# Attention, expert layer and MLP on one core: the conversion of doubles moved between engines, the first expert started in blocks of 128 tokens

## The chip, the cores and the metric

One core of a Trainium2 chip runs the whole program. The engines are TensorE (PE in the profile; PEld is its weight load), VectorE (DVE), ScalarE (ACT), GpSimd (POOL) and SyncE (SP), which issues most DMAs. Each runs its own instructions in order. The metric is the device time of one execution in microseconds (us); lower is better.

## The reference, cut to what matters

```python
def reference(**kwargs):
...
    attn_out = _attn_ref(**attn_kwargs)
    B, H, S, D = attn_out.shape
    x = np.ascontiguousarray(attn_out.transpose(0, 2, 1, 3)).reshape(B * S, H * D)
    x = _moe_ref(x=x, **moe_kwargs)
    return _moe2_ref(x=x, **moe2_kwargs)
```

Attention has batch 4, 8 heads, 768 positions of 64 features; a query sees 96 local and 8 global keys, with a linear bias. Its rows (3072 tokens of 512 features) are dealt to 8 experts of 384 tokens each by a greedy rule over the gate's logits; an expert is `relu(x @ w1) @ w2` with 1024 hidden features. A last MLP (`w_in`, a leaky relu with its own slope per feature, `w_out`, 2048 hidden features) runs over all tokens. The results of the random generators times constants are doubles for `w_in` and `w_out`, so these two arrive in 64 bits and the kernel makes float32 of them.

## The kernel before, in words

**Attention and conversion.** `attention` goes through 24 tiles of 128 queries, each in two steps of four heads (u = 0 and 1), so through 48 steps, and a step's parts are written in an order by hand. In step n: DMA issues for later tiles on SP; `place_globals` copies the global keys into the key columns of step n + 2 (POOL, L190); `place_values` copies the global values into rows of the value tile before (POOL, L196); then scores of step n + 1 (PE L212, DVE L218, ACT L221), the transposes of the probabilities (PE L232, copies on DVE L236 and ACT L234), the divisor (POOL L259), the combination of step n - 2 (PE L277, DVE), transposes of keys or queries for a later tile (PE L169, ACT L174 or L178), and last the product with the values of step n - 1 (PE L248).

Beside it runs `Doubles`, a generator of 32 jobs that turns 128x512 doubles into floats. `turn(n)` gives it four steps of five, two calls of `next(side)` in such a step. At the first call `begin` puts the shifted and limited high word into `t` (ACT L73, POOL L74) and the scaled low word into `r` (POOL L75), and `finish` splits the job before into a high and a low part if it belongs to `w_in`, every second job (POOL L87, L88). At the second call, the step's end, `join` packs the bits (DVE L79, L80) and adds the low word (POOL L82). `t` and `r` have two buffers, the raw tile three; the load of a raw tile is issued in `begin`'s call, two jobs ahead.

**Router and experts.** After attention the `Router` searches for the expert and its 384 tokens by counting above thresholds (DVE, with small matmuls). It is a generator too, and `filler` (L404) is a row of bf16 matmuls whose result nobody reads, put on PE between. `Experts.run` gathers the first expert's rows in three indirect DMAs of 128 tokens (POOL), transposes them (PE L857), splits them into a high and a low part (ACT L872, DVE L873), and runs the products in three passes (high by high, high by low, low by high). The first layer is `up1` (L923), with its relu on ACT and DVE (L926, L927), then `down1` (L950). Weights are split by `split` (ACT L890, POOL L891). Only the first expert's start is changed; later experts are transposed inside the previous expert's second layer (`up2` L963, `down2` L988).

The loop that sets the step's order:

```python
            if n + 2 < N:
                place_globals(*steps[n + 2])
            place_values(g, u)
            if turn(n):
                next(side)
            if nx:
                scores(*nx)
...
        if turn(n):
            next(side)
        else:
            next(setup, None)
```

Of the kernel before, what the change touches and what calls it, by code (L numbers as in the profile page):

```python
# [9 lines left out]
FT = mybir.dt.float32  # L10
FR = mybir.dt.float32r
BF = mybir.dt.bfloat16
I32 = mybir.dt.int32
U32 = mybir.dt.uint32
U16 = mybir.dt.uint16
AF = mybir.ActivationFunctionType
OP = mybir.AluOpType
# [13 lines left out]
class Doubles:  # L31
# [37 lines left out]
    def begin(self, job):  # L69
        nc, raw = self.nc, job["raw"]  # L70
        t = job["t"] = self.pool.tile([128, self.WIDTH], I32, name="f64_t")
        r = job["r"] = self.pool.tile([128, self.WIDTH], I32, name="f64_r")
        nc.scalar.activation(t.bitcast(FT), raw[:, :, 1].bitcast(FT), AF.Abs, scale=LIFT)  # L73
        nc.gpsimd.tensor_scalar(t.bitcast(FT), t.bitcast(FT), BIG, FLOOR, op0=OP.min, op1=OP.max)  # L74
        nc.gpsimd.tensor_scalar(r, raw[:, :, 0].bitcast(U32), 2.0 ** -29, 1.0, op0=OP.mult, op1=OP.mult)  # L75

    def join(self, job):
        nc, t = self.nc, job["t"]
        nc.vector.tensor_scalar(t, t, 3, 0x7FFFFFF8, op0=OP.logical_shift_left, op1=OP.bitwise_and)  # L79
        nc.vector.scalar_tensor_tensor(t, job["raw"][:, :, 1], -0x80000000, t, op0=OP.bitwise_and, op1=OP.bitwise_or)  # L80
        dst = t if job["dst"] is None else job["dst"].bitcast(I32)
        nc.gpsimd.tensor_tensor(dst, t, job["r"], op=OP.add)  # L82

# [7 lines left out]
def attention(ctx, tc, q, k, v, w_gate, n_global, n_local, ident, x_dram, logits, side, router):  # L91
# [212 lines left out]
    def turn(n):  # L304
        return 2 <= n < N - 3 and n % PACE[1] < PACE[0]
# [14 lines left out]
    for n in range(N + 2):  # L320
        if n < N:
# [8 lines left out]
            if n + 2 < N:  # L330
                place_globals(*steps[n + 2])
            place_values(g, u)
            if turn(n):
# [20 lines left out]
        if n >= N:  # L354
            combine(*steps[n - 2])
        if turn(n):
            next(side)
        else:
            next(setup, None)


class Router:
# [236 lines left out]
    def phase(self, k, result):  # L599
# [116 lines left out]
        if wide:  # L716
            self.filler(5120)
        yield
# [80 lines left out]
class Experts:  # L799
# [86 lines left out]

    def split(self, name, e, f, shape):
        r = self.st.pop(("r" + name, e, f))
        s = self.pair("m_s" + name, shape, 2)
        self.nc.scalar.activation(s[:, 0], r, AF.Copy)  # L890
        self.nc.gpsimd.tensor_tensor(s[:, 1], r, s[:, 0], op=OP.subtract)  # L891
        self.st["s" + name, e, f] = s
# [22 lines left out]
    def up1(self, e, f):  # L915
        nc = self.nc
        s1 = self.st.pop(("s1", e, f))
        x = self.ex[e]["x"]
        n = self.NT * 128
        ps = self.hidden.tile([128, 512], FT, name="m_h", bufs=3)  # L920
        for d in range(self.ND):
            for i, (a, b) in enumerate(self.PASSES):
                nc.tensor.matmul(ps[:, :n], s1[:, a, d], x[:, b, d], start=(d == 0 and i == 0),  # L923
                                 stop=(d == self.ND - 1 and i == 2))
        h = self.pair("m_hh", [n], 2)
        nc.scalar.activation(h[:, 0], ps[:, :n], AF.Relu)  # L926
        nc.vector.scalar_tensor_tensor(h[:, 1], ps[:, :n], 0.0, h[:, 0], op0=OP.max, op1=OP.subtract)  # L927
        self.st["h", e, f] = h

    @staticmethod  # L930
# [75 lines left out]
    def run(self, router, n_experts):  # L1006
# [15 lines left out]
        self.load_rest(0)  # L1022
        self.split_w1(0, 0)
        next(gen)
        ps = [self.acc.tile([128, 512], FT, name="m_acc", bufs=4) for _ in range(self.ND)]
        for a in range(self.NT):
            for d in range(self.ND):
                self.transpose(ps[d], 0, a, d)
        for d in range(self.ND):
            self.x_split(ps[d], 0, d)  # L1030
        self.split_w1(0, 1)
# [13 lines left out]

        self.up1(0, 0)
        next(gen)
# [133 lines left out]
```

## Time and profile before

| what | value |
|---|---|
| runs of the kernel before | 1121.75 us median of 3 (1120.18 to 1121.84) |
| the profiled execution | 1119.95 us, its span 1118.2 us |
| busy share of the span | PE 95%, PEld 84%, DVE 68%, POOL 48%, ACT 34% |
| mean granted TensorE clock | 0.976 of full speed |

The span runs from the first to the last instruction; the profiled execution's time holds 1.75 us more that lies around it. PE is busy nearly everywhere, but the matmuls' ends are modelled, and PE can be slow while busy: PEclk tells the clock that it was granted. The share of an engine over the whole span mixes attention, where DVE, POOL and ACT are well filled, with the expert part, where PE is.

### The profile page before, as it was taken

What the parts mean: (1) busy time and instruction counts of PE and PEld (TensorE: products, weight loads), DVE (VectorE), ACT (ScalarE), POOL (GpSimd) and SP (SyncE); (2) the same over time, 40 slices, a digit from 0 to 9 for tenths busy, and PEclk for the clock granted to TensorE, in tenths of its full rate; (3) what the DMA queues carried; (4) which work ended last, traced back from release to release, by engine and by line L of the source; (5) the groups of instructions that cost most, each with busy time, mean ns of one, the idle gap of its engine ahead of it and who ended that gap; (6) DMA issues with size and microseconds to landing.
All of it is one profiled execution on the core that took longest, in us unless ns stands there. A gap on an engine that the chain in (4) does not pass through costs nothing.

```text
span 1118.2 us, 19406 instructions
## 1 busy us (share of the span) xinstructions
PE 1065.7 (95%) x6659; PEld 944.2 (84%) x6659; DVE 762.9 (68%) x2228; ACT 385.6 (34%) x969; POOL 540.5 (48%) x652
## 2 busy tenths in 40 slices
PE   8989898869999999999999999999999999999997
PEld 6777677648888998899889988898899999999995
DVE  7989888778897878897789698778753323231321
ACT  7777777503322320232133113211331233123211
POOL 4888878315455823462346325432543354236222
PEclk9999999968999999999999999999999999999999
DMA  9788877114135525441534533533353435434131
GB/s 219 212 218 223 209 202 187 49 46 134 57 132 179 173 83 181 130 160 58 198 96 149 163 123 109 157 135 129 95 180 123 133 108 185 131 116 167 57 131 67
DMA packets 151219, 156.55 MB, mean 140 GB/s; under 512 B 83536, under 2 KB 116304, under 8 KB 151120
## 3 DMA queue, kind: packets, MB, share of 16 engines
q1 hardware_dynamic: 147280, 142.72, 42.3%
q0 software_dynamic: 3840, 12.59, 3.4%
q8 instruction: 53, 0.87, 0.3%
q14 instruction: 46, 0.38, 0.1%
HBM read 134.31 MB, written 20.97 MB: 139 GB/s over the span
## 4 chain that ended last, share of the span: by engine, by line
PE 75%; DVE 12%; POOL 6%; issue 3%; ACT 2%; DMA 2%; SPq 0%; DVEq 0%; POOLq 0%; ACTq 0%
PE m_h L963 23%; PE m_acc L988 23%; PE m_h L923 9%; PE m_acc L950 9%; PE a_s L212 2%; PE a_pt L232 2%; PE a_xp L248 2%; DVE r_thr L564 2%; DVE r_red L778 1%; DVE r_cmp L770 1%; PE r_ps L704 1%; POOL wo L82 1%; ACT a_p L221 1%; PE a_cb L277 1%; PE a_tp L169 1%
## 5 line engine op out<-in xcount | busy, mean ns | idle before, releaser
L973 POOL TENSOR_TENSOR m_g<-m_t,m_g 128x384 fp32r<-128x384 f32 (+1 forms) x144 | 140.2, 973 | 372.1 <-ACT m_g L972 369.1
L988 PE MATMUL m_acc<-m_so,m_g 128*128 128x512 f32 x1152 | 298.7, 399 | 0.4 <-POOL m_spacer L996 0.3
L963 PE MATMUL m_h<-m_y,wi 128*128 128x384 f32 x1536 | 294.4, 341 | 0.0
L963 PEld LDWEIGHTS m_h<-m_y,wi 128*128 128x128 f32 x1536 | 273.3, 189 | 7.5
L988 PEld LDWEIGHTS m_acc<-m_so,m_g 128*128 128x128 f32 x1152 | 209.6, 189 | 35.3 <-POOL m_g L973 0.9
L972 ACT ACTIVATE m_g<-m_t 128x384 fp32r<-128x384 f32 (+1 forms) x144 | 70.5, 490 | 435.6 <-DVE m_t L971 255.1
L891 POOL TENSOR_TENSOR m_s<-m_r,m_s 128x512 fp32r<-128x512 f32 x128 | 166.9, 1308 | 103.5 <-ACT m_s L890 103.2
L970 DVE TENSOR_SCALAR m_t<-m_h,m_al 128x384 f32<-128x384 f32 (+1 forms) x144 | 82.2, 571 | 149.2 <-PE m_h L963 136.1
L950 PE MATMUL m_acc<-m_hh,m_s 128*128 128x384 f32 x768 | 150.3, 340 | 1.3 <-DVE m_hh L927 1.3
L923 PE MATMUL m_h<-m_xt,m_s 128*128 128x384 f32 x768 | 146.1, 338 | 0.0
L923 PEld LDWEIGHTS m_h<-m_xt,m_s 128*128 128x128 f32 x768 | 136.4, 190 | 1.9 <-ACT m_xt L872 0.3
L950 PEld LDWEIGHTS m_acc<-m_hh,m_s 128*128 128x128 f32 x768 | 132.4, 188 | 2.9 <-DVE m_hh L927 1.6
L890 ACT ACTIVATE m_s<-m_r 128x512 fp32r<-128x512 f32 x128 | 79.7, 626 | 98.8 <-PE m_acc L950 34.1
L221 ACT ACTIVATE a_p<-a_sx,a_mn 128x232 f32<-128x232 f32 (+1 forms) x192 | 88.5, 462 | 25.8 <-DVE a_mn L218 25.4
L927 DVE SCALAR_TENSOR_TENSOR m_hh<-m_h,m_hh 128x384 fp32r<-128x384 f32 x64 | 35.4, 552 | 76.8 <-ACT m_hh L926 76.2
L971 DVE SCALAR_TENSOR_TENSOR m_t<-m_h,m_t 128x384 f32<-128x384 f32 (+1 forms) x144 | 73.9, 513 | 4.9
L778 DVE TENSOR_REDUCE r_red<-r_cmp 128x24 bf16<-128x576 bf16 (+1 forms) x97 | 73.9, 761 | 3.4
L218 DVE CUSTOM_DVE_ANT_0 a_sx<-a_s,a_bias 128x232 f32<-128x232 f32 (+1 forms) x192 | 61.4, 374 | 11.6 <-PE a_s L212 9.4
L212 PE MATMUL a_s<-a_kz,a_qz 64*128 64x232 f32 (+1 forms) x384 | 50.2, 381 | 18.7 <-POOL a_kz L190 16.2
L926 ACT ACTIVATE m_hh<-m_h 128x384 fp32r<-128x384 f32 x64 | 31.5, 492 | 95.6 <-PE m_h L923 82.3
L770 DVE TENSOR_TENSOR r_cmp<-r_mk,r_thr 128x576 bf16<-128x576 uint16 x78 | 61.4, 787 | 0.0
L212 PEld LDWEIGHTS a_s<-a_kz,a_qz 64*128 64x128 f32 x384 | 33.2, 193 | 28.6 <-POOL a_kz L190 22.6
(183 smaller groups left out, 1283.3 us busy)
## 6 DMA issues: line engine op xcount, KB each, us to landing
m_so<-wo_pairs SPq DMA_DIRECT2D x112, 512.0 KB, 3.3
m_r<-in_moe_w_dram SPq DMA_DIRECT2D x128, 256.0 KB, 3.0
f_raw<-in_moe_w_in_dram SPq DMA_DIRECT2D x16, 512.0 KB, 4.6
f_raw<-in_moe_w_out_dram SPq DMA_DIRECT2D x16, 512.0 KB, 3.7
wo_pairs<-m_so SPq DMA_DIRECT2D x16, 512.0 KB, 2.6
a_k<-in_k_dram SPq DMA_DIRECT2D x24, 256.0 KB, 4.8
a_q<-in_q_dram SPq DMA_DIRECT2D x24, 256.0 KB, 5.2
a_v<-in_v_dram SPq DMA_DIRECT2D x24, 256.0 KB, 4.8
```

The source lines that it names most:

```text
L212: nc.tensor.matmul(ps[s][:, a, :n], T["Q", g][r, p], kz[r, p, c0:c0 + n], start=True, stop=True)
L221: nc.scalar.activation(pr[:, s, 2 * C - n:], sx[:, s, :n], AF.Exp, bias=T["mn", g][:, h:h + 1], scale=-1.0, accum_out=T["sum", g][:, h:h + 1])
L778: nc.vector.tensor_reduce(red, cmp, axis=AX.X, op=OP.add)
L890: self.nc.scalar.activation(s[:, 0], r, AF.Copy)
L891: self.nc.gpsimd.tensor_tensor(s[:, 1], r, s[:, 0], op=OP.subtract)
L923: nc.tensor.matmul(ps[:, :n], s1[:, a, d], x[:, b, d], start=(d == 0 and i == 0), stop=(d == self.ND - 1 and i == 2))
L950: nc.tensor.matmul(ps[:, :n], s2[:, b, d * 128:(d + 1) * 128], h[:, a], start=(f == 0 and a + b == 0), stop=(last and a == 1))
L963: nc.tensor.matmul(ps[:, :n], self.wi[:, a, d, f * 128:(f + 1) * 128], y[:, b, d], start=(d == 0 and i == 0), stop=(d == self.ND - 1 and i ...
L970: nc.vector.tensor_scalar(t[:, cs], ps[:, cs], 0.0, self.al[:, f:f + 1], op0=OP.min, op1=OP.mult)
L971: nc.vector.scalar_tensor_tensor(t[:, cs], ps[:, cs], 0.0, t[:, cs], op0=OP.max, op1=OP.add)
L973: nc.gpsimd.tensor_tensor(g[:, 1, cs], t[:, cs], g[:, 0, cs], op=OP.subtract)
L988: nc.tensor.matmul(ps, g[:, a, t * 128:(t + 1) * 128], s[:, b], start=(f == 0 and a + b == 0), stop=(last and a == 1))
```

## The change

Four things change. In `Doubles`, the scaling of the low word is an ACT pass that writes back into the raw tile, `r` is gone, the add reads the raw tile, and `t` has three buffers. In `attention`, `place_values` is called at the step's end, ahead of the second call of the side work. In the router one row of filler is 6144 columns long instead of 5120. And the first expert's start is a function of its own, `first_up`: each block of 128 tokens is transposed into one bank, split in one pass, and multiplied by itself in 12 matmuls of 128 columns; two fillers of 512 columns stand between; the first split of `w1` has its subtraction on DVE, and the router's next step and the other splits come after.

```diff
--- before.py
+++ after.py
@@ -68,18 +68,17 @@
 
     def begin(self, job):
         nc, raw = self.nc, job["raw"]
-        t = job["t"] = self.pool.tile([128, self.WIDTH], I32, name="f64_t")
-        r = job["r"] = self.pool.tile([128, self.WIDTH], I32, name="f64_r")
+        t = job["t"] = self.pool.tile([128, self.WIDTH], I32, name="f64_t", bufs=3)
         nc.scalar.activation(t.bitcast(FT), raw[:, :, 1].bitcast(FT), AF.Abs, scale=LIFT)
         nc.gpsimd.tensor_scalar(t.bitcast(FT), t.bitcast(FT), BIG, FLOOR, op0=OP.min, op1=OP.max)
-        nc.gpsimd.tensor_scalar(r, raw[:, :, 0].bitcast(U32), 2.0 ** -29, 1.0, op0=OP.mult, op1=OP.mult)
+        nc.scalar.activation(raw[:, :, 0], raw[:, :, 0].bitcast(U32), AF.Copy, scale=2.0 ** -29)
 
     def join(self, job):
         nc, t = self.nc, job["t"]
         nc.vector.tensor_scalar(t, t, 3, 0x7FFFFFF8, op0=OP.logical_shift_left, op1=OP.bitwise_and)
         nc.vector.scalar_tensor_tensor(t, job["raw"][:, :, 1], -0x80000000, t, op0=OP.bitwise_and, op1=OP.bitwise_or)
         dst = t if job["dst"] is None else job["dst"].bitcast(I32)
-        nc.gpsimd.tensor_tensor(dst, t, job["r"], op=OP.add)
+        nc.gpsimd.tensor_tensor(dst, t, job["raw"][:, :, 0], op=OP.add)
 
     def finish(self, job):
         if job["hi"] is not None:
@@ -329,7 +328,6 @@
             nx = steps[n + 1] if n + 1 < N else None
             if n + 2 < N:
                 place_globals(*steps[n + 2])
-            place_values(g, u)
             if turn(n):
                 next(side)
             if nx:
@@ -353,6 +351,8 @@
             router.start()
         if n >= N:
             combine(*steps[n - 2])
+        if n < N:
+            place_values(g, u)
         if turn(n):
             next(side)
         else:
@@ -714,7 +714,7 @@
         ps = self.psum.tile([128, 512], FT, name="r_ps")
         nc.tensor.matmul(ps[:, :3], lists.rearrange("p g s -> p (g s)"), self.unit, start=True, stop=True)
         if wide:
-            self.filler(5120)
+            self.filler(6144)
         yield
         idx = w.tile([128, 3], I32, name="r_idx", bufs=8)
         nc.vector.tensor_copy(idx, ps[:, :3])
@@ -884,11 +884,11 @@
         self.nc.sync.dma_start(r, src[:, f, :])
         self.st["r2", e, f] = r
 
-    def split(self, name, e, f, shape):
+    def split(self, name, e, f, shape, engine=None):
         r = self.st.pop(("r" + name, e, f))
         s = self.pair("m_s" + name, shape, 2)
         self.nc.scalar.activation(s[:, 0], r, AF.Copy)
-        self.nc.gpsimd.tensor_tensor(s[:, 1], r, s[:, 0], op=OP.subtract)
+        (engine or self.nc.gpsimd).tensor_tensor(s[:, 1], r, s[:, 0], op=OP.subtract)
         self.st["s" + name, e, f] = s
 
     def split_w1(self, e, f):
@@ -922,10 +922,49 @@
             for i, (a, b) in enumerate(self.PASSES):
                 nc.tensor.matmul(ps[:, :n], s1[:, a, d], x[:, b, d], start=(d == 0 and i == 0),
                                  stop=(d == self.ND - 1 and i == 2))
+        self.relu(ps, e, f)
+
+    def relu(self, ps, e, f):
+        nc, n = self.nc, self.NT * 128
         h = self.pair("m_hh", [n], 2)
         nc.scalar.activation(h[:, 0], ps[:, :n], AF.Relu)
         nc.vector.scalar_tensor_tensor(h[:, 1], ps[:, :n], 0.0, h[:, 0], op0=OP.max, op1=OP.subtract)
         self.st["h", e, f] = h
+
+    def first_up(self, filler):
+        nc = self.nc
+        s1 = self.st.pop(("s1", 0, 0))
+        x = self.ex[0]["x"] = self.pair("m_xt", [self.ND, self.NT * 128], 1)
+        out = self.hidden.tile([128, 512], FT, name="m_h", bufs=3)
+
+        def part(a):
+            return slice(a * 128, (a + 1) * 128)
+
+        def turn(a):
+            ps = self.acc.tile([128, 512], FT, name="m_acc", bufs=4)
+            for d in range(self.ND):
+                nc.tensor.transpose(ps[:, part(d)], self.ex[0]["xr"][a][:, part(d)], self.ident)
+            ps = ps.rearrange("p (d t) -> p d t", t=128)
+            hi, lo = x[:, 0, :, part(a)], x[:, 1, :, part(a)]
+            nc.scalar.activation(hi, ps, AF.Copy)
+            nc.vector.tensor_tensor(lo, ps, hi, op=OP.subtract)
+
+        def multiply(a):
+            todo = [(d, i, j) for i, j in self.PASSES for d in range(self.ND)]
+            todo.sort(key=lambda m: m[2])
+            for n, (d, i, j) in enumerate(todo):
+                nc.tensor.matmul(out[:, part(a)], s1[:, i, d], x[:, j, d, part(a)], start=(n == 0),
+                                 stop=(n == len(todo) - 1))
+
+        turn(0)
+        filler(512)
+        turn(1)
+        multiply(0)
+        turn(2)
+        multiply(1)
+        filler(512)
+        multiply(2)
+        self.relu(out, 0, 0)
 
     @staticmethod
     def order(n, last):
@@ -1020,14 +1059,8 @@
         nc.gpsimd.iota(behind, pattern=[[0, 1]], base=0, channel_multiplier=0)
         nc.sync.value_load(behind[0:1, 0:1], min_val=0, max_val=1)
         self.load_rest(0)
-        self.split_w1(0, 0)
-        next(gen)
-        ps = [self.acc.tile([128, 512], FT, name="m_acc", bufs=4) for _ in range(self.ND)]
-        for a in range(self.NT):
-            for d in range(self.ND):
-                self.transpose(ps[d], 0, a, d)
-        for d in range(self.ND):
-            self.x_split(ps[d], 0, d)
+        self.split("1", 0, 0, [self.ND, 128], nc.vector)
+        self.first_up(router.filler)
         self.split_w1(0, 1)
         self.split_w2(0, 0)
         self.split_w2(0, 1)
@@ -1043,7 +1076,7 @@
             else:
                 self.split_w2(e, 1)
 
-        self.up1(0, 0)
+        next(gen)
         next(gen)
         self.split_w1(0, 2)
         chosen = fetched = 0
```

POOL, in attention, two steps in a row of which the second finishes a `w_in` job (a_kz the keys with the global ones placed, a_v the values, a_se the divisor, f_t and f_r the two words of a job, wi and wo the resident weights). Before:

```order
L259 TENSOR_SCALAR a_se<-a_sum 128x4
L190 COPY a_kz<-a_kg 128x2x8
L196 COPY a_v<-a_vg 32x256
L74 TENSOR_SCALAR f_t<-f_t 128x512
L75 TENSOR_SCALAR f_r<-f_raw 128x512
L87 TENSOR_SCALAR wi<-f_t 128x512
L88 TENSOR_TENSOR wi<-f_t,wi 128x512
L259 TENSOR_SCALAR a_se<-a_sum 128x4
L82 TENSOR_TENSOR wo<-f_t,f_r 128x512
```

With the change (line numbers are one less):

```order
L258 TENSOR_SCALAR a_se<-a_sum 128x4
L195 COPY a_v<-a_vg 32x256
L189 COPY a_kz<-a_kg 128x2x8
L73 TENSOR_SCALAR f_t<-f_t 128x512
L86 TENSOR_SCALAR wi<-f_t 128x512
L87 TENSOR_TENSOR wi<-f_t,wi 128x512
L258 TENSOR_SCALAR a_se<-a_sum 128x4
L195 COPY a_v<-a_vg 32x256
L81 TENSOR_TENSOR wo<-f_t,f_raw 128x512
```

The copy into a_v has moved behind the divisor, right ahead of the add of the same step, and the instruction that made f_r is gone; the add reads f_raw.

PE, the first expert's start (m_x gathered rows, m_xt their split transposes, m_s a split weight, m_acc and m_h PSUM banks). Before:

```order
L857 MATMUL m_acc<-ident,m_x 128x128 x12
L923 MATMUL m_h<-m_xt,m_s_4034 128x384 x12
L786 LDWEIGHTS r_ones
L786 MATMUL r_ps<-r_red,r_ones 128x24
L923 MATMUL m_h<-m_xt,m_s_4076 128x384 x12
```

With the change:

```order
L946 MATMUL m_acc<-ident,m_x 128x128 x4
L404 LDWEIGHTS r_ones
L404 MATMUL m_h<-r_slots,r_ones 128x512
L946 MATMUL m_acc<-ident,m_x 128x128 x4
L956 MATMUL m_h<-m_xt,m_s_4004 128x128 x12
L946 MATMUL m_acc<-ident,m_x 128x128 x4
L956 MATMUL m_h<-m_xt,m_s_4004 128x128 x12
L404 LDWEIGHTS r_ones
L404 MATMUL m_h<-r_slots,r_ones 128x512
L956 MATMUL m_h<-m_xt,m_s_4004 128x128 x12
```

The twelve transposes and twelve wide matmuls have become three times four transposes and three times twelve narrow ones, the second block's transposes ahead of the first block's matmuls, with a filler (L404) in two places.

ACT at the same place (m_r a loaded weight tile, m_hh the hidden rows). Before:

```order
L890 ACTIVATE m_s_4034<-m_r_3927 128x512
L872 ACTIVATE m_xt<-m_acc 128x384 x4
L890 ACTIVATE m_s_4076<-m_r_3931 128x512
L890 ACTIVATE m_s_4079<-m_r_3929 128x512
L890 ACTIVATE m_s_4082<-m_r_4028 128x512
L926 ACTIVATE m_hh<-m_h 128x384
```

With the change:

```order
L890 ACTIVATE m_s_4004<-m_r_3895 128x512
L949 ACTIVATE m_xt<-m_acc 128x4x128 x3
L930 ACTIVATE m_hh<-m_h 128x384
L890 ACTIVATE m_s_4073<-m_r_3899 128x512
L890 ACTIVATE m_s_4076<-m_r_3897 128x512
L890 ACTIVATE m_s_4079<-m_r_3998 128x512
```

The relu (m_hh) now stands ahead of the three splits of the next weights, which stood ahead of it before.

## Rows read from the trace of the kernel before

**Rows 1.** Windows, five attention steps each: length, busy us per engine, clock, DMA, GB/s.
```profile
114.70:136.63 21.93, 17.84 (x169) 14.22 (x165) 18.86 (x75) 16.65 (x55) 18.66 (x31) 1.00 0.83 218
...
sum 179.83, PE 160.83 PEld 132.49 DVE 154.71 ACT 137.32 POOL 149.96; mean PE 20.10 PEld 16.56 DVE 19.34 ACT 17.17 POOL 18.75
```

**Rows 2.** Timeline, DVE, first score reduction of four steps: start us, us, engine.
```profile
118.15 0.40 DVE L218 CUSTOM_DVE_ANT_0 a_sx<-a_s,a_bias 128x232 f32<-128x232 f32 x1 [1.01 <-PE a_s L212]
...
122.41 0.39 DVE L218 CUSTOM_DVE_ANT_0 a_sx<-a_s,a_bias 128x232 f32<-128x232 f32 x1
...
131.13 0.39 DVE L218 CUSTOM_DVE_ANT_0 a_sx<-a_s,a_bias 128x232 f32<-128x232 f32 x1
...
136.63 0.39 DVE L218 CUSTOM_DVE_ANT_0 a_sx<-a_s,a_bias 128x232 f32<-128x232 f32 x1
```

**Rows 3.** Waits, 40 to 206 us: us in total, times, longest.
```profile
PEld a_s L212 <- POOL a_kz L190: 22.1, 18, 3.0
ACT a_p L221 <- DVE a_mn L218: 20.8, 26, 2.0
ACT f_t L73 <- POOL wi L88: 20.5, 11, 3.1
...
POOL a_v L196 <- PE a_xp L248: 2.7, 4, 0.9
```

**Rows 4.** Readers of the raw doubles, 40 to 206 us: ns minimum/median/maximum.
```profile
L75 POOL TENSOR_SCALAR f_r<-f_raw x29: 659/681/954, 39.4 to 197.4; 128x512 int32<-128x512 uint32 x29
L80 DVE SCALAR_TENSOR_TENSOR f_t<-f_raw,f_t x29: 691/1020/1643, 40.4 to 197.8; 128x512 int32<-128x512 int32 x29
L73 ACT ACTIVATE f_t<-f_raw x28: 654/674/703, 42.6 to 193.7; 128x512 f32<-128x512 f32 x28
```

**Rows 5.** Timeline, PE, one attention step.
```profile
138.36 1.05 PE L212 MATMUL a_s<-a_kz,a_qz 64*128 64x232 f32 x8
...
140.28 0.66 PE L277 MATMUL a_cb<-a_cmb,a_xt 128*128 128x144 f32 x4
140.77 0.60 PE L169 MATMUL a_tp<-ident,a_k 128*128 128x128 f32 x4
...
142.32 1.05 PE L212 MATMUL a_s<-a_kz,a_qz 64*128 64x232 f32 x8
```

**Rows 6.** Timeline, PE, the first expert's start.
```profile
252.52 0.95 PE L857 MATMUL m_acc<-ident,m_x 128*128 128x128 f32 x4 [0.95 <-DMA m_x<-x_rows,r_idx]
254.08 1.11 PE L857 MATMUL m_acc<-ident,m_x 128*128 128x128 f32 x4 [0.61 <-DMA m_x<-x_rows,r_idx]
255.14 4.48 PE L923 MATMUL m_h<-m_xt,m_s 128*128 128x384 f32 x12
...
259.51 2.37 PE L923 MATMUL m_h<-m_xt,m_s 128*128 128x384 f32 x12
261.72 1.72 PE L950 MATMUL m_acc<-m_hh,m_s 128*128 128x384 f32 x9
```

**Rows 7.** Timeline, ACT and POOL, the same stretch.
```profile
256.09 1.69 ACT L890 ACTIVATE m_s<-m_r 128x512 fp32r<-128x512 f32 x3
259.65 0.49 ACT L926 ACTIVATE m_hh<-m_h 128x384 fp32r<-128x384 f32 x1 [1.87 <-PE r_ps L786]
...
256.82 3.77 POOL L891 TENSOR_TENSOR m_s<-m_r,m_s 128x512 fp32r<-128x512 f32 x3 [4.37 <-ACT m_s L890]
```

**Rows 8.** Windows, the first expert's start.
```profile
253.00:256.00 3.00, 2.39 (x9) 1.35 (x8) 1.59 (x4) 1.41 (x4) 0.00 (x0) 0.50 0.85 234
```

**Rows 9.** Timeline, PE, the second layer of a later expert.
```profile
563.58 2.37 PE L963 MATMUL m_h<-m_y,wi 128*128 128x384 f32 x12
565.79 1.55 PE L988 MATMUL m_acc<-m_so,m_g 128*128 128x512 f32 x6
567.18 0.19 PE L786 MATMUL r_ps<-r_red,r_ones 128*128 128x24 bf16 x1
```

**Rows 10.** Windows, from the first expert's second product to the end.
```profile
261.72:1118.20 856.48, 842.48 (x4569) 764.77 (x4568) 550.94 (x1390) 216.63 (x422) 369.01 (x353) 0.99 0.39 130
```

## The prediction

> **What bounds the kernel now.** I read the windows view first. From the first expert's second product on, PE is busy in 842.5 of 856.5 us [rows 10]. The change touches nothing in that last part, and nothing there can move but PE's own work, so I take its 856.5 us as they are. What can move lies before it: attention with the conversion of the doubles, and the first expert's start.
>
> In attention I cut the time into groups of five steps, because a conversion job runs in four steps of five. Eight groups take 179.83 us, 22.48 each [rows 1]. No engine is full: the means are PE 20.1, DVE 19.3, POOL 18.75, ACT 17.2. The steps are unequal: one takes 4.26 us (118.15 to 122.41), another 5.50 (131.13 to 136.63) [rows 2]. The waits tell who makes the long ones: ACT waits 20.5 us in all for POOL's low-part subtraction L88 before it may write the next t (two buffers), and PE's weight loads wait 22.1 us for the key copies L190 that stand behind that work in POOL's queue [rows 3]. A job whose two parts are written out puts L74, L75, L87, L88 and L82 on POOL in one step; POOL falls behind, ACT stands at L73 ahead of the exponentials, and the next step is long.
>
> At the first expert's start PE transposes three blocks of gathered rows as they land, waits for the split of x, and runs its first product, 12 matmuls, from 255.14 to 259.51 [rows 6]. It does so at a granted clock of 0.50, the 1.2 GHz level [rows 8]; the second product takes 2.21 us, half as long, at 259.51 [rows 6].
>
> **Attention, part by part.** (1) The multiplication of the low words leaves POOL, 0.681 us at the median, and comes to ACT as a pass like L73, 0.674 us [rows 4]. The trace has no such ACT pass with integers, so L73, the same shape and the same stride, is its price. Per group of four jobs POOL goes from 18.75 to 16.0 us, ACT from 17.17 to 19.9. (2) DVE's L80 takes 0.691 us at best and 1.020 at the median [rows 4]; part of that is POOL beside it. With less on POOL, DVE's 19.3 falls to between 18.0 (four times 0.33 less) and 19.3. (3) The third t buffer lets L73 write while the job two before is still being split: the 20.5 us wait of ACT goes. What is late next is ACT itself, now the fullest with 19.9. (4) The copy of the values waits at the head of POOL's step for PE's product, 2.7 us in all [rows 3]; at the end of the step that product is past, and the wait is covered. Behind it in the queue now stands only the add L82, which waits for DVE anyway; the values are needed one step later, so I price the move at nothing; if PE's product were late again, it would cost those 2.7 us. (5) On SP the load of a raw tile now waits for POOL's add, not for DVE's L80, about 1.3 us later; it is needed two jobs, some 8 us, on. Nothing, unless it holds k, q and v behind it (a rival below).
>
> What is a group then? PE's dense step is 3.96 us (138.36 to 142.32) [rows 5], five of them 19.8. I take a step with a job at 4.26, the step of [rows 2] in which nobody stood long, and the fifth at PE's 3.96: 4 x 4.26 + 3.96 = 21.0. That leaves ACT 1.1 us of slack in a group, which is tight. The gain is 22.48 - 21.0 = 1.48, times 8 groups **-11.8 us**. Ends: ACT's 19.9 as the whole group gives -20.6; if 32 new passes, 21.6 us, stay on the path and only the wait of 20.5 goes, +1.1. I stay nearer the good end since three of the four steps of [rows 2] already run at 4.26 to 4.36 (122.41 to 131.13 are two).
>
> Here a rule of the Trainium skill speaks about (2). The row shows L80 0.33 us above its best at the median [rows 4]. The page "SBUF — State Buffer", where it reads the diagram of the ports, says that VectorE with two SBUF inputs and GpSimd lock one another out for whole instructions. By it the removed 0.681 could give DVE up to 4 x 0.681 = 2.7 us a group, and the sum would be at the good end, -20.6; the constant 0.33 does not look like it, and no step here shows it alone.
>
> **The first expert's start.** (6) The fillers of 6144 columns are two matmuls more, while PE only waits for rows: nothing. (7) The first product becomes 36 matmuls of 128 columns instead of 12 of 384, block by block. No such narrow product in this number format is in the trace. By columns: 384 take 2.21/12 = 0.184 us and 512 take 1.39/6 = 0.232 [rows 9], so 128 would take 0.088. By the nearest width in plain fp32: two 144-wide products take 0.49 us [rows 5], 0.218 for 128. I take 0.218, since width is what changes here and only that row has it. The second block's rows are transposed by about 253.1. Then 12 x 0.218 gives 255.7, the third block's transposes 256.2, twelve more 258.8, a filler 259.0, twelve more 261.6, against 259.51 before [rows 6]: +2.1 us. This is at the full clock, 2.4 GHz: the fillers and the early blocks leave fewer gaps than the transposes alone did; that the clock stays up no row can tell. (8) The split of w1 for the second product moves behind the relu on ACT. Before, ACT did three splits in 1.69 us at 256.09 and POOL three subtractions in 3.77 at 256.82, all under the slow first product, and the relu came at 259.65 [rows 7]. Now POOL's part is done only about 2.6 us after the first product (relu 0.4, split 0.56, subtraction 1.26, and 0.35 for three hand-overs, estimated from the gaps between those rows), and PE can do two matmuls before: a new stall of 2.2 us. The down product's own split is then ready in time. (9) The first split's subtraction on DVE runs while rows are on their way: nothing. (10) The router's next pass on DVE comes after the relu; PE reaches its total only after the second product, covered. Sum **+4.3 us**. Ends: with 0.088 the first product ends at 257.0, so -2.5 + 2.2 = -0.3; with 0.218 and the half clock up to 259.5 as before, 6.4 us do 3.2 of 8.55 us of work, the end is 264.9, +7.5.
>
> **Sum.** -11.8 + 4.3 = -7.5. The profiled execution took 1119.95 us (span 1118.2), so 1112.45; the median of the runs is 1.80 above it: **1114.2 us**.
>
> **Rivals.**
> - The narrow products go by columns (0.088). For it: 384 and 512 lie on one line [rows 9]. Then -11.8 - 0.3 = -12.1, 1109.7 us. The Trainium skill, "TensorE: Matmul & The Clock Gate", section on the back-to-back issue gap, gives 81 ns for a 128-column matmul with its weight load, without naming this number format; by that, as an estimate, the start comes at -0.5 and the time at 1109.5.
> - The raw loads hold ACT: SP stands for POOL's add, k, q, v and the next doubles come later, and half of the gain goes: -5.9 + 4.3 = -1.6, 1120.2 us. Against it: 8 us of lead.
> - Slower: ACT becomes the bound. It waits 20.8 us for DVE's score reductions [rows 3], 2.8 us in each of the 7.4 groups of that stretch. If those waits stay as they are, since the reductions depend on PE and DVE and not on POOL, ACT's group is 19.9 + 2.8 = 22.7, 0.2 more than now, eight times +1.6, and with the start +5.9: 1127.7 us. It decides from the point where ACT's waits stay above 2.6 us a group. Against it: much of that waiting follows from POOL's late key copies, which hold PE.
>
> **How the numbers follow.** Forecast 0.62, products by columns 0.18, late loads 0.11, ACT as the bound 0.09. About 0.2%, 2.2 us, is what a measurement of this kernel can tell from no change, so "same" is 1119.5 to 1124.0. Faster: nearly all of the forecast, all of the second and a part of the third case, 0.80; slower: the last, 0.09; between, 0.11. The range of 1106 to 1120.5 us takes in the two faster cases, attention 3 to 4 us better or 6 worse than taken, and the late loads; it leaves out the ACT case and the far ends.
>
> **What would show it.** Right: ACT's L73 no longer waits for the subtraction; groups of five at about 21 us with no step over 5; ACT over 90% busy in them; PE idle some 2 us in front of the third matmul of the second product, waiting for POOL; narrow products about 0.21 us apart. Wrong: groups still at 22.4 with ACT waiting for DVE; narrow products under 0.1 us apart; waits of L73 for the raw loads; or a half clock all through the first product.

## The result and the profile after

The change gives 1110.26 us (median of 4 runs, 1109.04 to 1115.36) against 1121.34 for the kernel before beside it (4 runs, 1120.18 to 1121.84): a ratio of 0.9906, 95% interval 0.988 to 0.9933. The forecast was 1114.2. The profiled execution took 1111.46 us.

The page of the kernel after, the span and the busy share of each engine:

```profile
span 1109.7 us, 19448 instructions
...
PE 1061.6 (96%) x6685; PEld 942.4 (85%) x6687; DVE 757.2 (68%) x2228; ACT 401.4 (36%) x1000; POOL 516.2 (47%) x619
```

The span is 8.5 us shorter. Where that comes from is read from PE's timeline at the first expert's start. The kernel before, its first gathered block:

```profile
250.91 0.66 PE L857 MATMUL m_acc<-ident,m_x 128*128 128x128 f32 x4 [0.89 <-DMA m_x<-x_rows,r_idx]
```

The kernel after, the same stretch of PE. Here L946 are the transposes, L956 the narrow products, L786 the router's count, L923 the second product and L989 the down product. The first block's transposes begin at 235.56:

```profile
238.03 0.66 PE L946 MATMUL m_acc<-ident,m_x 128*128 128x128 f32 x4 [1.60 <-DMA m_x<-x_rows,r_idx]
238.44 1.54 PE L956 MATMUL m_h<-m_xt,m_s 128*128 128x128 f32 x12
239.81 0.62 PE L946 MATMUL m_acc<-ident,m_x 128*128 128x128 f32 x4
...
241.61 1.64 PE L956 MATMUL m_h<-m_xt,m_s 128*128 128x128 f32 x12
248.02 0.20 PE L786 MATMUL r_ps<-r_red,r_ones 128*128 128x24 bf16 x1 [4.77 <-DVE r_red L778]
248.12 4.18 PE L923 MATMUL m_h<-m_xt,m_s 128*128 128x384 f32 x12
252.09 2.70 PE L989 MATMUL m_acc<-m_hh,m_s 128*128 128x384 f32 x9
```

And the windows of the kernel after, from the first block on (length, busy us of PE, PEld, DVE, ACT and POOL, granted clock, DMA share, GB/s):

```profile
235.56:238.44 2.88, 1.28 (x9) 0.90 (x10) 0.69 (x1) 0.60 (x1) 0.38 (x2) 1.00 0.65 190
238.44:243.25 4.81, 4.81 (x44) 4.64 (x42) 1.38 (x2) 1.20 (x2) 0.00 (x0) 1.00 0.70 207
243.25:248.02 4.77, 0.00 (x0) 0.00 (x1) 4.11 (x9) 2.56 (x5) 3.65 (x3) 0.93 0.00 0
248.02:252.09 4.07, 4.07 (x13) 4.07 (x14) 2.92 (x9) 0.00 (x0) 1.51 (x2) 0.50 0.86 253
252.09:1109.70 857.61, 843.23 (x4569) 765.98 (x4568) 543.55 (x1385) 216.68 (x422) 367.80 (x352) 0.99 0.39 129
```

| stretch | before us | after us | difference |
|---|---|---|---|
| up to the first block on PE | 250.91 | 235.56 | -15.35 |
| first block to the end of the first product (before: with the count, 0.09) | 8.60 | 7.69 | -0.91 |
| PE idle ahead of the count L786 | 0 | 4.77 | +4.77 |
| second product (after: with the count, 0.10) | 2.21 | 4.07 | +1.86 |
| from the first down product to the end | 856.48 | 857.61 | +1.13 |
| sum | 1118.20 | 1109.70 | -8.50 |

The two ends of the first product before, 259.51 and 261.72, are in [rows 6], the rest of 856.48 us in [rows 10]. So attention gains 15.4 us, and the first expert's start with what follows it gives 6.9 of them back.

**Attention after.** The windows of the eight groups of five steps, the fourth and fifth of them and the sum row:

```profile
86.54:106.87 20.33, 20.24 (x206) 16.85 (x204) 19.67 (x78) 19.13 (x60) 15.75 (x25) 1.00 0.86 221
106.87:126.88 20.01, 18.18 (x175) 14.43 (x173) 18.63 (x75) 18.66 (x59) 15.34 (x26) 1.00 0.99 253
...
sum 164.11, PE 154.85 PEld 126.94 DVE 153.93 ACT 151.87 POOL 126.41; mean PE 19.36 PEld 15.87 DVE 19.24 ACT 18.98 POOL 15.80
```

A group takes 20.51 us, 22.48 before [rows 1]; 8 x 1.97 = 15.7 us, about the first line of the table. POOL has gone from 18.75 to 15.80 a group, ACT from 17.17 to 18.98. PE, DVE and ACT are now each busy for 92 to 94% of the group.

The granted clock rose too: between 24 and 184 us from a mean of 0.96 to 1.00, and every group after the change ran at 1.00. The gain is as large without it. Two groups ran at 1.00 before as well, the fifth, shown in [rows 1], and the fourth:

```profile
92.22:114.70 22.48, 21.52 (x215) 17.29 (x216) 19.93 (x78) 17.28 (x56) 18.91 (x30) 1.00 0.82 214
```

The same steps now take 20.33 and 20.01 us, so these two gained 2.15 and 1.92, and the mean of all eight is 1.97. The waits between 40 and 200 us:

```profile
ACT a_p L220 <- DVE a_mn L217: 14.1, 19, 2.4
PEld a_s L211 <- POOL a_kz L189: 11.9, 14, 2.1
POOL f_t L73 <- ACT f_t L72: 10.6, 7, 2.0
```

ACT's wait for the subtraction has no row any more, and the weight loads' wait for the key copies is about half of its 22.1 us [rows 3]. POOL, which held both, now waits itself, for ACT's shifted word. Both passes of ACT cost what was priced, and the median of DVE's bit packing is down to its best value [rows 4]:

```profile
L79 DVE SCALAR_TENSOR_TENSOR f_t<-f_raw,f_t x28: 691/693/1646, 40.6 to 179.8; 128x512 int32<-128x512 int32 x28
...
L74 ACT ACTIVATE f_raw<-f_raw x27: 670/694/726, 40.7 to 176.7; 128x512 int32<-128x512 uint32 x27
```

But DVE won nothing by that. The groups of instructions on DVE in attention (busy us, mean ns, idle before), first of the kernel before:

```profile
L80 DVE SCALAR_TENSOR_TENSOR f_t<-f_raw,f_t 128x512 int32<-128x512 int32 x29 | 28.0, 965 | 1.0
...
L79 DVE TENSOR_SCALAR f_t<-f_t 128x512 int32<-128x512 int32 x29 | 14.9, 515 | 11.2 <-POOL f_t L74 11.1
```

and of the kernel after:

```profile
L79 DVE SCALAR_TENSOR_TENSOR f_t<-f_raw,f_t 128x512 int32<-128x512 int32 x29 | 23.7, 817 | 1.0
L78 DVE TENSOR_SCALAR f_t<-f_t 128x512 int32<-128x512 int32 x29 | 20.5, 706 | 1.4 <-POOL f_t L73 1.4
```

The two passes of a job together took 965 + 515 = 1480 ns and now take 817 + 706 = 1523. What the second pass got back, the first now pays beside the POOL work that is left, while its idle time ahead of that pass fell from 11.2 to 1.4 us. One of the slow first passes, and POOL's subtraction beside it:

```profile
80.69 1.48 DVE L78 TENSOR_SCALAR f_t<-f_t 128x512 int32<-128x512 int32 x1
80.60 1.28 POOL L87 TENSOR_TENSOR wi<-f_t,wi 128x512 fp32r<-128x512 f32 x1
```

The pass ends at 82.17, 0.29 us after the subtraction; the same pass takes 0.42 us at 85.40, where no subtraction stands beside it.

**The stall at the count.** DVE in the kernel after, from the relu's second half to the next count:

```profile
243.81 0.56 DVE L931 SCALAR_TENSOR_TENSOR m_hh<-m_h,m_hh 128x384 fp32r<-128x384 f32 x1 [2.01 <-ACT m_hh L930]
...
244.69 1.04 DVE L564 SCALAR_TENSOR_TENSOR r_thr<-r_dig,r_step 128x72 uint16<-128x72 f32 x1
...
245.76 1.41 DVE L770 TENSOR_TENSOR r_cmp<-r_mk,r_thr 128x576 bf16<-128x576 uint16 x1
247.21 0.75 DVE L778 TENSOR_REDUCE r_red<-r_cmp 128x24 bf16<-128x576 bf16 x1
...
249.65 0.46 DVE L770 TENSOR_TENSOR r_cmp<-r_mk,r_thr 128x576 bf16<-128x576 uint16 x1
250.15 0.75 DVE L778 TENSOR_REDUCE r_red<-r_cmp 128x24 bf16<-128x576 bf16 x1
```

The router's pass stands behind the relu in program order, so DVE begins it at 244.28, and its last reduction ends at 247.96. PE has the count of that pass ahead of the second product in its queue, so PE stands still from 243.25 to 248.02. In the kernel before, the same pass ran while PE waited for rows: its last reduction, at 252.81, ended at 253.56, before the third block's transposes. POOL works at the late splits beside it:

```profile
244.38 5.15 POOL L891 TENSOR_TENSOR m_s<-m_r,m_s 128x512 fp32r<-128x512 f32 x4 [8.41 <-ACT m_s L890]
```

The comparison L770 takes 1.41 us there, and 0.46 once POOL is done at 249.53.

### The profile page after: what moved, and what is told of

It is laid out like the page before. It is cut to its first block, busy times and chain, and to the rows that moved or that the text cites. A ratio compares the mean times of both kernels' runs of the same rounds, so it can differ in the third digit from the quotient of the medians.

```text
span 1109.7 us, 19448 instructions
## 1 busy us (share of the span) xinstructions
PE 1061.6 (96%) x6685; PEld 942.4 (85%) x6687; DVE 757.2 (68%) x2228; ACT 401.4 (36%) x1000; POOL 516.2 (47%) x619
## 3 DMA queue, kind: packets, MB, share of 16 engines
q1 hardware_dynamic: 147280, 142.72, 42.9%
## 4 chain that ended last, share of the span: by engine, by line
PE 75%; DVE 12%; ACT 3%; issue 2%; DMA 1%; POOL 1%; SPq 0%; DVEq 0%; ACTq 0%; POOLq 0%
PE m_h L1002 24%; PE m_acc L1027 23%; PE m_acc L989 11%; PE m_h L923 10%; DVE a_sx L217 2%; ACT a_p L220 1%; DVE r_thr L564 1%; PE a_xp L247 1%; PE r_ps L704 1%; DVE r_red L778 1%; PE a_s L211 1%; PE a_pt L231 1%; DMA m_x<-x_rows,r_idx 1%; DVE r_cmp L770 1%; DVE f_t L78 1%
## 5 line engine op out<-in xcount | busy, mean ns | idle before, releaser
L989 PE MATMUL m_acc<-m_hh,m_s 128*128 128x384 f32 x768 | 151.1, 342 | 1.2 <-DVE m_hh L931 1.2
L923 PE MATMUL m_h<-m_xt,m_s 128*128 128x384 f32 x756 | 143.6, 338 | 0.0
L989 PEld LDWEIGHTS m_acc<-m_hh,m_s 128*128 128x128 f32 x768 | 133.6, 190 | 2.9 <-DVE m_hh L931 1.5
L923 PEld LDWEIGHTS m_h<-m_xt,m_s 128*128 128x128 f32 x756 | 134.3, 190 | 1.2
L770 DVE TENSOR_TENSOR r_cmp<-r_mk,r_thr 128x576 bf16<-128x576 uint16 x78 | 61.5, 789 | 0.0
L211 PE MATMUL a_s<-a_kz,a_qz 64*128 64x232 f32 (+1 forms) x384 | 49.0, 375 | 9.3 <-POOL a_kz L189 8.6
L231 PE MATMUL a_pt<-ident,a_p 128*128 128x128 f32 x352 | 49.9, 282 | 0.2
```

The costliest lines, as they stand in the source:

```text
L989: nc.tensor.matmul(ps[:, :n], s2[:, b, d * 128:(d + 1) * 128], h[:, a], start=(f == 0 and a + b == 0), stop=(last and a == 1))
```

## Experiments

The theory after the result: all of attention's gain comes from the pass that left POOL; the third buffer and the moved copy give nothing; and the start loses by the order of two calls, the router's pass and the second product's split behind the blocks. The rivals: that the third buffer, which removes a wait of 20.5 us, is the gain; and that the start loses by the narrow products or the clock alone. The lines quoted are those of each kernel, so numbers shift by one or two. The experiments ran in three groups, each beside its own runs of the kernel before: the first four (1119.92 us), the next four (1119.55) and the last two (1120.09). Kernels of different groups, and the change itself (beside 1121.34), are compared by their distance to these.

**All three attention edits, the old start.**

```diff
 kernel before, with the edits of Doubles and attention
-        t = job["t"] = self.pool.tile([128, self.WIDTH], I32, name="f64_t")
-        r = job["r"] = self.pool.tile([128, self.WIDTH], I32, name="f64_r")
+        t = job["t"] = self.pool.tile([128, self.WIDTH], I32, name="f64_t", bufs=3)
...
-        nc.gpsimd.tensor_scalar(r, raw[:, :, 0].bitcast(U32), 2.0 ** -29, 1.0, op0=OP.mult, op1=OP.mult)
+        nc.scalar.activation(raw[:, :, 0], raw[:, :, 0].bitcast(U32), AF.Copy, scale=2.0 ** -29)
...
-        nc.gpsimd.tensor_tensor(dst, t, job["r"], op=OP.add)
+        nc.gpsimd.tensor_tensor(dst, t, job["raw"][:, :, 0], op=OP.add)
...
-            place_values(g, u)
...
+        if n < N:
+            place_values(g, u)
```

> The kernel before with the three attention edits and the old start. Theory (attention gives 15.4 us, the start takes some 7 back): the first gathered block lands about 15.4 us earlier than before's 250.91, and the whole is 13 to 16 us faster than before, so faster than the changed kernel by 5 to 7. Rival (the start is a gain or neutral): within 1 us of the changed kernel or slower.

1104.76 us (1104.05 to 1105.73, 4 runs) against 1119.92; ratio 0.9869, interval 0.9851 to 0.9887. PE's timeline of this kernel, from the first block:

```profile
235.71 0.66 PE L857 MATMUL m_acc<-ident,m_x 128*128 128x128 f32 x4 [0.87 <-DMA m_x<-x_rows,r_idx]
...
239.87 4.40 PE L923 MATMUL m_h<-m_xt,m_s 128*128 128x384 f32 x12
244.11 0.19 PE L786 MATMUL r_ps<-r_red,r_ones 128*128 128x24 bf16 x1
244.15 2.33 PE L923 MATMUL m_h<-m_xt,m_s 128*128 128x384 f32 x12
246.31 1.72 PE L950 MATMUL m_acc<-m_hh,m_s 128*128 128x384 f32 x9
```

The first block comes as early as with the whole change, and from it to the down product take 10.60 us instead of 252.09 - 235.56 = 16.53. In these two profiles the new start costs 5.9 us. By the medians this kernel lies 15.2 us under the kernel before and the change 11.1, a difference of 4.1; the two intervals of the ratio overlap by a little.

**The low word's pass alone.**

```diff
 kernel before
-        r = job["r"] = self.pool.tile([128, self.WIDTH], I32, name="f64_r")
...
-        nc.gpsimd.tensor_scalar(r, raw[:, :, 0].bitcast(U32), 2.0 ** -29, 1.0, op0=OP.mult, op1=OP.mult)
+        nc.scalar.activation(raw[:, :, 0], raw[:, :, 0].bitcast(U32), AF.Copy, scale=2.0 ** -29)
...
-        nc.gpsimd.tensor_tensor(dst, t, job["r"], op=OP.add)
+        nc.gpsimd.tensor_tensor(dst, t, job["raw"][:, :, 0], op=OP.add)
```

> Only the low word's scaling goes to ACT; t keeps two buffers, the values stay at the step's front. Theory (the loop from POOL's L88 through the t buffer to ACT's pass makes the long steps, and 0.68 us less on POOL shortens the loop): 6 to 11 us faster than before, ACT still waits for L88, 5 us or more in all. Rival 1 (only POOL's load counts): the full 15. Rival 2 (only the buffer counts): under 2 us.

1104.22 us (1103.31 to 1104.57, 4 runs); ratio 0.9863, interval 0.9846 to 0.988. The whole gain, with two buffers and the copy in its old place: the theory's 6 to 11 us were too few, and the rival that only POOL's load counts held. Its waits, 40 to 206 us:

```profile
ACT a_p L220 <- DVE a_mn L217: 7.3, 14, 1.3
ACT f_t L72 <- POOL wi L87: 6.6, 7, 1.8
```

ACT still waits for the subtraction, and pays that much less for DVE: 7.3 + 6.6 = 13.9 us, while with all three edits the wait for DVE alone is 13.9. The one wait seems to stand in for the other; the equal sums are all that shows it.

**The third buffer alone** (the scaling stays on POOL, and writes in place).

```diff
 kernel before
-        t = job["t"] = self.pool.tile([128, self.WIDTH], I32, name="f64_t")
-        r = job["r"] = self.pool.tile([128, self.WIDTH], I32, name="f64_r")
+        t = job["t"] = self.pool.tile([128, self.WIDTH], I32, name="f64_t", bufs=3)
...
-        nc.gpsimd.tensor_scalar(r, raw[:, :, 0].bitcast(U32), 2.0 ** -29, 1.0, op0=OP.mult, op1=OP.mult)
+        nc.gpsimd.tensor_scalar(raw[:, :, 0], raw[:, :, 0].bitcast(U32), 2.0 ** -29, 1.0, op0=OP.mult, op1=OP.mult)
...
-        nc.gpsimd.tensor_tensor(dst, t, job["r"], op=OP.add)
+        nc.gpsimd.tensor_tensor(dst, t, job["raw"][:, :, 0], op=OP.add)
```

> t has three buffers; POOL still scales the low word, in place in the raw tile (r is dropped to make room). Theory: ACT's wait for L88 goes, but POOL stays at about 18.7 of each 22.5 us group and remains the late one: 2 to 6 us faster than before. Rival (the buffer wait is the whole cause): the full 15. Rival (POOL's load is the whole cause): under 1 us.

1122.57 us (1119.33 to 1124.2, 10 runs); ratio 1.0023, interval 1.0009 to 1.0038: no gain, rather a small loss, where the theory had 2 to 6 us of gain. Scaling in place takes POOL 0.792 us on average, 0.787 before, so the edit hides nothing there. Its waits, 40 to 206 us:

```profile
ACT a_p L220 <- DVE a_mn L217: 42.9, 31, 3.4
PEld a_s L211 <- POOL a_kz L189: 25.3, 20, 3.5
```

The 20.5 us are gone from L72, and all of it stands at the next instruction that needs the step's scores: 20.8 + 20.5 = 41.3 before [rows 3], 42.9 here. The keys still come late from POOL.

**The moved copy of the values alone.**

```diff
 kernel before
-            place_values(g, u)
             if turn(n):
...
+        if n < N:
+            place_values(g, u)
         if turn(n):
```

> Only the copy of the global values moves to the step's end. Theory: it covers a wait of 2.7 us in all on POOL: 0 to 3 us faster than before. Rival (it frees the long steps, since L74 starts without it): 5 us or more. Rival (it delays the add and the next key copy): slower by 1 us or more.

1118.4 us (1117.23 to 1119.61, 10 runs); ratio 0.9991, interval 0.9981 to 1.0: 0.1%, less than counts. The product with the values now waits for the copy in seven steps, which it did not before:

```profile
PE a_xp L248 <- POOL a_v L196: 6.7, 7, 1.3
```

**The router's pass ahead of the blocks.**

```diff
 kernel after
         self.split("1", 0, 0, [self.ND, 128], nc.vector)
+        next(gen)
         self.first_up(router.filler)
...
         next(gen)
-        next(gen)
         self.split_w1(0, 2)
```

> The changed kernel with one of the router's two steps back ahead of the first product, so that the next count is on DVE while the rows arrive. Theory (PE's 4.77 us of idling at the count's matmul L786, which stands ahead of the second product, is DVE's late count): that wait goes to under 0.5 us, the late split of w1 shows in its place with about 2.3 us, and the whole is 2.5 to 5 us faster than the changed kernel, the upper end if the clock stays up. Rival (the late split is the gate already, as the prediction had it): within 0.5 us.

1110.04 us (1108.03 to 1113.24, 6 runs); ratio 0.9913, interval 0.9899 to 0.9927, as the change itself. PE's timeline:

```profile
238.32 2.80 PE L956 MATMUL m_h<-m_xt,m_s 128*128 128x128 f32 x12
240.92 1.07 PE L946 MATMUL m_acc<-ident,m_x 128*128 128x128 f32 x4
...
247.16 0.24 PE L786 MATMUL r_ps<-r_red,r_ones 128*128 128x24 bf16 x1
248.45 1.01 PE L923 MATMUL m_h<-m_xt,m_s 128*128 128x384 f32 x2 [1.05 <-ACT m_s L890]
249.81 3.57 PE L923 MATMUL m_h<-m_xt,m_s 128*128 128x384 f32 x10 [0.35 <-POOL m_s L891]
```

The 4.77 us are gone, and the stall that the prediction had expected comes out from under them: 1.05 us for ACT's split, two matmuls, then 0.35 for POOL's part. In this execution the narrow products ran at the half clock, which took the rest of the gain: from the first block to the down product take 17.55 us. That PE waited for the router's pass is shown by this trace; the 2.5 to 5 us expected from moving it did not come.

**The second product's split ahead of the blocks.**

```diff
 kernel after
-        self.first_up(router.filler)
         self.split_w1(0, 1)
+        self.first_up(router.filler)
```

> The changed kernel with the split of w1 for the second product ahead of the first. Theory (the count's matmul is the gate): within 1 us of the changed kernel; PE still idles 3 us or more at L786, less than 4.77 only as far as DVE's count runs faster without POOL beside it. Rival (the split is the gate): 2 us faster or more.

1111.21 us (1107.18 to 1115.08, 6 runs); ratio 0.9917, interval 0.9895 to 0.994. The stall at the count is the same to the last digit, so the split is not what PE waits for. (The narrow products ran at the half clock here too, so the count comes later. POOL still has three other splits beside the router's pass, 249.06 to 252.98, and the comparison L770 takes 1.41 us as before.)

```profile
252.71 0.20 PE L786 MATMUL r_ps<-r_red,r_ones 128*128 128x24 bf16 x1 [4.77 <-DVE r_red L778]
```

**Both.** The edits of the last two together.

> Both moves. Theory: no wait over 0.5 us between the first and the second product, the second at the full clock in 2.2 us: 4.8 + 1.8 + 1.1 = 7.7 us faster than the changed kernel, some 18 to 19 faster than before. Rival (the clock falls anyway): 4 to 5 us faster than the changed kernel.

1105.51 us (1104.98 to 1110.61, 5 runs); ratio 0.9883, interval 0.9866 to 0.9901. PE's timeline:

```profile
242.99 0.19 PE L786 MATMUL r_ps<-r_red,r_ones 128*128 128x24 bf16 x1
243.03 2.35 PE L923 MATMUL m_h<-m_xt,m_s 128*128 128x384 f32 x12
245.22 2.08 PE L989 MATMUL m_acc<-m_hh,m_s 128*128 128x384 f32 x9
```

Neither stall is left, and the second product runs at the full clock. The median is 4.5 and 5.7 us under those of the two kernels with one move. Against the kernel before it gains 14.0 us, the change 11.1: 3.0 us more, where 7.7 were expected, and the two intervals overlap. The first block stands at 235.49, so from it to the down product take 9.73 us, 0.9 less than with the old start (10.60), whose first product ran at the half clock. More than that no profile here shows the blocks to be worth.

**No fillers between the blocks** (and the router's row at 5120 columns again).

```diff
 kernel after
-            self.filler(6144)
+            self.filler(5120)
...
         turn(0)
-        filler(512)
         turn(1)
...
         multiply(1)
-        filler(512)
         multiply(2)
```

> The changed kernel with the filler row back at 5120 columns and without the two fillers in the first expert's start. Theory (the fillers hold the clock for the narrow products): the first product's 36 matmuls run in part at 0.50 and end 1.5 to 4 us later. Rival (the early blocks themselves hold it): the same clock and time within 0.5 us. Third case: the narrow products end later but under the count's wait, which then hides it: no change of the whole.

1114.51 us (1111.22 to 1115.39, 6 runs); ratio 0.9943, interval 0.993 to 0.9956: 3.3 us over the kernel with the early split, beside which it ran and which has the same stall (4.77 us there, 4.78 here). The intervals overlap a little. That the fillers hold the clock for the narrow products is not shown: in the profiles of both kernels all of these ran at the half clock, and from the first block to the down product take 20.16 us without the fillers and 20.07 with them. The 2.2 us between the two profiles lie behind that.

**The low word's pass with the blocks and both moves, beside the low word's pass with the old start.** The edit is that of the second experiment on the kernel of the experiment "Both", whose third buffer and moved copy are undone.

> The low word's pass alone (two t buffers, the values' copy where it was), with the blocks of 128 and both the router's pass and the second product's split ahead of the blocks. Theory (the two attention edits beside the low word give nothing, and the blocks with both moves are worth what the old start is worth): 1104 to 1105.5 us, within 1 us of the kernel with the low word's pass and the old start. Rival (with the stalls gone, the blocks come out ahead, since their products run while the third block is on its way): 1102 to 1103.5 us, over 1 us below it.

> The low word's pass alone with the old start, again, beside the kernel above on one chip: 1103.3 to 1104.6 us, as in its first runs, by both theories.

With the blocks 1107.59 us (1105.55 to 1108.75, 5 runs), ratio 0.9881, interval 0.9858 to 0.9903; with the old start 1105.67 (1105.56 to 1106.98, 4 runs), ratio 0.9866, interval 0.9842 to 0.989. Neither theory had it: the blocks are not ahead, and 2 us behind in the median, though the intervals overlap; and the old start, run again, lies 1.1 us above the range expected for it. In the profiles the blocks take 14.86 us from the first block to the down product, the old start 10.64. The windows of the kernel with the blocks tell why:

```profile
230.00:234.00 4.00, 3.65 (x22) 1.66 (x20) 3.00 (x12) 1.01 (x2) 1.52 (x2) 1.00 0.60 184
...
238.00:240.00 2.00, 2.00 (x12) 2.00 (x11) 1.97 (x5) 0.60 (x1) 0.00 (x0) 0.50 0.86 241
```

and those of the kernel "Both", with the same start:

```profile
230.00:234.00 4.00, 4.00 (x12) 1.43 (x12) 3.41 (x12) 1.26 (x2) 1.93 (x2) 0.58 0.59 170
...
238.00:240.00 2.00, 1.29 (x12) 1.15 (x12) 1.76 (x4) 0.29 (x1) 0.00 (x0) 1.00 0.85 261
```

In the one the half clock (0.50) falls on the narrow products, behind a stretch of fillers at 1.00; in the other it falls on the fillers ahead (0.58), whose result nobody reads, and the products run at 1.00. The start is the same. No kernel here is shown to be ahead of the simplest: the low word's pass alone, 1.3 to 1.4% under the kernel before in two sets of runs.

## Why the prediction was right, and where not

**The sum.** In the profiled execution 1112.45 was forecast and 1111.46 measured. The parts were off by more, in opposite directions: attention -15.35 instead of -11.8, the start +6.9 instead of +4.3. That the sum came so near is luck in part: the two errors, 3.6 and 2.6 us, have opposite signs. The forecast of the median lies 3.9 us high, of which 1.0 is this, 1.8 was added for the standing of the first profile to its median, and 1.2 is that this profile stands above its own.

**(1) the ACT pass:** its price was right, 0.694 us against 0.674. What it adds to a group was taken too high: 2.7 us were added, and ACT went from 17.17 to 18.98, by 1.8. For one thing, a pass starts before the one ahead has ended (L72 at 69.52 for 0.66 us, L74 already at 70.08). So ACT was less near to being the bound than was feared, and its wait for DVE fell to 14.1 us, about 1.8 a group, under the 2.6 from which the third rival would have decided.

**The group.** 21.0 us were forecast, and it takes 20.51; ACT is over 90% busy in it, as was said, and so are PE and DVE. The step of 4.26 us under the sum was no rule: the two steps of the forecast that are said to run at 4.36 take 4.08 and 4.64 (the score reductions stand at 122.41, 126.49 and 131.13), and 4.36 is their mean. After the change steps take from 2.6 to 5.3 us, and five of forty are over 5, against the sign that none would be; before it were seven. The dense step of PE was read rightly: three in a row take 3.96 us (L211, from 88.67 to 100.55).

**(2) DVE:** the step failed in its end, not in the sum. L80's median fell to its best, but DVE's two passes together did not get shorter (1480 and 1523 ns), so DVE stayed at 19.2 a group, next to the upper of the two bounds. By the exclusive lock of the Trainium skill, "SBUF — State Buffer", section "SBUF: two separate sides", the prediction had an estimate of 2.7 us a group; the trace shows 0.1 (19.34 to 19.24), since the remaining POOL instructions hold DVE's first pass instead, as the pair at 80.6 us above shows for one case.

**(3) the third buffer:** wrong as a cause. That "the 20.5 us wait of ACT goes" is true and was worth nothing: alone it moved the wait to the exponentials, and without it the gain is whole. The prediction read this wait of ACT as what makes the step long; it was a place where ACT stood for what POOL delivered late anyway. That a wait on another row was part of the same lateness was even said in the third rival ("much of that waiting follows from POOL's late key copies"), which is the sentence that held.

**(4), (5) the copy and the raw loads:** nothing, as forecast; no wait of L72 for a raw load is in the trace.

**(6) the fillers:** priced at nothing; without them the median was 3.3 us higher, with intervals that overlap, and the two profiles put none of it into the start.

**(7) the narrow products:** mis-sized, and the truth lay nearer to the first rival. At the full clock twelve take 1.37 us (238.44 to 239.81), 0.114 each, between 0.088 and 0.218. The end of the first product came 0.9 us nearer to the first block, where +2.1 was forecast, and -2.5 by the rival. The value taken was that of another number format; the rows of the same format, in width 384 and 512, were nearer. The plain fp32 row itself would have told: it counts four matmuls for the kernel's two products [rows 5], so one of them takes 0.49/4 = 0.12 us, and 0.109 for 128 columns. The Trainium skill's 81 ns for 128 columns ("TensorE: Matmul & The Clock Gate", the back-to-back issue gap) lies below all that was measured.

**(8) the late split:** there, but smaller than the 2.2 us forecast, and hidden: 1.4 us, seen only once the pass was moved.

**(10) the router's pass:** this step failed. "PE reaches its total only after the second product, covered" is contradicted by the order of PE that stands ahead of the prediction: L786 is the row between the two L923. The pass was moved from under PE's wait for rows to behind the relu, and everything behind it on PE paid 4.77 us. A step moved on DVE was followed to its place on DVE, and not to the instruction that reads its result on PE's queue.

**The clock** of the start was bounded in the range and not forecast in place: the second product ran at 0.50 behind the stall, +1.8 us without the count, and the down product's first nine matmuls, begun at 0.50, took 2.54 us instead of 1.74. With the stall gone ("Both") the second product ran at 1.00. The rest of the table's last line, 0.3 us, says nothing: from the first down product on all kernels run the same code, and in the twelve profiles that stretch took 854.4 to 858.1 us.

**What stays open.** No run tells what puts the half clock on the fillers in one execution and on the products in another. Of the six profiles with the blocks, two (the change and "Both") have it on the fillers, and PE comes to the count behind them without a wait; in the other four the fillers ran at the full clock, PE stood 1.0 to 1.5 us ahead of that count, and the narrow products ran at the half. So the 0.114 us of (7) is what two profiles of six show.

## What to carry to other kernels

A wait that is long in the table is worth nothing if what ends it is late for all: ask first whose work is late, and take work off that engine; one buffer more only moves the waiting. When a call is moved, follow its result to the reader's queue, and look at what stands behind that reader. Price an unknown width from the same format before the same width of another, and count the instructions that a row stands for.

## What the runs showed of the hardware that was not expected

- A product of 128 columns in this format took 0.114 us at a granted clock of 1.00 and 0.217 at 0.50 (twelve from 238.32 to 240.92 with the router's pass moved). The value taken for the full clock, 0.218, was by chance that of the half. A product in plain fp32 stands in the trace as two matmuls (the 144-wide row of [rows 5]), in this format as one.
- DVE's comparison of two arrays took 1.41 us beside POOL's subtraction and 0.46 without; its reduction of one array 0.75 in both places. That agrees with the Trainium skill, "SBUF — State Buffer", section on who interferes with whom: two inputs from SBUF contend with GpSimd, a reduction never does.
- One and the same start of the first expert spread over 1107.2 to 1115.1 us in six runs (the early split), while the low word's pass with the old start spread over less than 2 us (1104.05 to 1105.73, 1103.31 to 1104.57 and 1105.56 to 1106.98, four runs each). Two profiles of the same blocks differ by where the half clock falls; that it does the same in the other runs is an inference. The old start alone does not make the runs agree: the kernel before spread over 3.9 us in 19 runs, and with the third buffer over 4.9 in ten.
